# The transfers of the last two blocks' turned results: from two queues to one

## The chip, the cores and the metric

The kernel runs on one core of a Trainium2 chip. The metric is the device time of one execution in microseconds (us). Before the change it is 588.04 us, the median of 3 runs (587.76 to 588.65).

## The reference

Attention over packed keys, and then a channel mix on what it gives. Eight batches of 8 heads, 576 tokens and 64 values per head are read; 4608 tokens of 512 channels are written.

```python
p_packed = sm_attn(p, k, v)                 # 32 packed rows attend to 576 tokens
x = sm_attn(q, p_packed, p_packed)          # 576 tokens attend to the 32 rows
# x: (8, 576, 512) after the heads are put side by side
xk = mu_k * x + (1.0 - mu_k) * x_prev       # x_prev: the token before
xr = mu_r * x + (1.0 - mu_r) * x_prev
k = np.maximum(xk @ w_k, 0.0)               # 512 -> 1024
v = k * k @ w_v                             # 1024 -> 512
r = 1.0 / (1.0 + np.exp(-(xr @ w_r)))       # 512 -> 512
return (r * v).astype(np.float32)
```

## The kernel before

The 4608 tokens are cut into nine blocks of 512. Blocks 0 to 6 go through the channel mix one after the other (gates, keys, values), and their results have tokens on the partitions, so that each goes to `out` in rows. The last two blocks (`PAIR`, blocks 7 and 8) are worked on together: keys and values of the pair are made in seven products of halves in place of eight, and in these the channels are on the partitions and the 512 tokens along the free dimension. So a result of theirs must be turned before it can be written.

That end of the kernel is `values_of_pair` (L1716). Its table `passes` (from L1777) has seven passes named A11, S2, S3, S1, A12, S4 and A22. A pass fills two PSUM banks (j = 0 and 1) with 12 matmuls each: 4 chunks of weights, and for each chunk a product of high parts and two with a low part (L1802 to L1804). Four of the passes (S1, A12, S4 and A22) end in results, two each, so there are eight results of 128 channels by 512 tokens. `made_of` (L1734) makes a result. In S1, A12 and S4 VectorE adds a kept partial sum to the bank (L1747), multiplies by the gate (L1750) and turns the result in blocks of 32 by 32 (L1752) back into the tile of the gate. In the last pass, A22, there is no partial sum to add (`n is None`); the gate is multiplied in (L1741), and the turned result goes to another tile, `turned`.

A turned result leaves in four transfers (a = 0 to 3), one for each 32 partitions: 32 partitions of 16 runs of 32 numbers, so 64 KB in 512 runs of 128 bytes. `to` and `what` in the code are their two ends. `load` (L215) issues a transfer on SyncE's queue (SP in the profile, L221). ScalarE (ACT) has a queue of its own, on which L1761 issues.

What sets the order. The kernel is written as generators, which the class `Flow` runs (L149). A generator yields an engine and an estimated time, and the planner goes on with the one that can start earliest on its engine by its own count of times. The instructions of an engine come out in the order in which the planner emits them, and each engine takes its own strictly in that order. For transfers `Flow` keeps a count named "queue", which is SP's, and one named "dma". The transfers that L1761 issues are entered under "scalar". A transfer raises a semaphore when its data has landed. There are eight of these for the transfers of SP and ACT together (DMAHW0 to DMAHW7 in the order below), dealt in turn in the order of emission, and before a transfer is issued its engine waits until the one that had the same semaphore before has landed.

Of the kernel before, what the change touches and what calls it, by code (L numbers as in the profile page):

```python
# [173 lines left out]
def attn_pack_channel_mix(ctx: ExitStack, tc: tile.TileContext, q, k, v, p, mu_k, mu_r, w_k, w_v, w_r, out):  # L174
    nc = tc.nc
# [24 lines left out]
    def vec(n, after=None):  # L200
        return "vector", 0.07 + 1.04e-3 * n, after, None
# [4 lines left out]
    def act(n, after=None, table=None):  # L206
        return "scalar", 0.14 + 0.72e-3 * n, after, table
# [4 lines left out]
    def pe(us, after=None):  # L212
        return "tensor", us, after, None

    def load(dst, src, issue, us, beside=False):  # L215
        if beside:
            yield "gpsimd", 0.6, None, None
            nc.gpsimd.dma_start(dst, src)
            return
        yield "queue", issue, None, None  # L220
        nc.sync.dma_start(dst, src)  # L221
        begin = max(flow.free.get("dma", 0.0), flow.t + 0.46)
        flow.free["dma"] = begin + us
        flow.free["queue"] = max(flow.free["queue"], begin - 2.0)
        flow.now.t = begin + us + LANDS
# [27 lines left out]
    def banks(slot):  # L253
        return ps.tile([P, 2, 512], F32, name="pa", tag=f"pa{slot}")
# [186 lines left out]
    def back_to_issue():  # L441
        flow.now.t = flow.free["queue"]
# [905 lines left out]
    def small_tile(slot, dtype, name):  # L1348
        tag, j = slot
        o = LEAD[tag][j]  # L1350
        return tile_([P, S], dtype, tag, j, name)[:, o:o + WP]
# [364 lines left out]
    def values_of_pair():  # L1716

        first, second = PAIR
        ms = []
        for _ in range(4):  # L1720
            ms.append((yield from flow.take("m")))
        Z, Y = ([ps.tile([P, TB], F32, name="pv", tag=f"m{slot}") for slot in ms[n:n + 2]] for n in (0, 2))
        X = [None, None]
        parts_of = {}

        def kept(n, j):
            slot = yield from flow.take("keep")
            x = small_tile(slot, F32, "kept")
            parts_of[n, j] = slot, x
            yield act(TB)  # L1730
            nc.scalar.copy(x, Z[j])
            flow.set(("kept v", n, j))

        def made_of(bank, j, i, h, n):  # L1734
            yield from flow.wait(("sig", i, 2 * h + j))
            sig = sigs[i, 2 * h + j]
            if n is None:
                slot = yield from flow.take("keep")
                x = small_tile(slot, F32, "turned")
                yield vec(TB)  # L1740
                nc.vector.tensor_tensor(sig, bank[j], sig, op=ALU.mult)  # L1741
                sig, x = x, sig
            else:
                yield from flow.wait(("kept v", n, j))
                slot, x = parts_of[n, j]
                yield vec(TB)
                nc.vector.tensor_tensor(x, bank[j], x, op=ALU.add)  # L1747
                flow.set(("read v", n, j))
                yield vec(TB)
                nc.vector.tensor_tensor(x, x, sig, op=ALU.mult)  # L1750
            yield vec(TB)
            nc.vector.transpose(sig.rearrange("p (a b) -> p a b", b=32), x.rearrange("p (a b) -> p a b", b=32))  # L1752
            if n is not None:
                flow.give("keep", slot)
            for a in range(4):
                d = DH * h + P * j + 32 * a
                to = out[i * TB:(i + 1) * TB, d:d + 32].rearrange("(b k) i -> k b i", k=32)
                what = sig[32 * a:32 * a + 32].rearrange("k (b i) -> k b i", i=32)
                if n is None and a % 2:
                    yield "scalar", 0.1, None, None  # L1760
                    nc.scalar.dma_start(to, what)  # L1761
                else:
                    yield from load(to, what, 0.5, 0.3)
                    back_to_issue()

        def of_wv(f0, o):
            return lambda u, j: tuple(wvs[f0 + u][:, x, o + j * P:o + (j + 1) * P] for x in range(2))

        def of_wr(home):
            flat = home.rearrange("p c d -> p (c d)").rearrange("p (h u d) -> p h u d", h=2, u=HF)  # L1770
            return lambda u, j: tuple(flat[:, x, u, j * P:(j + 1) * P] for x in range(2))

        def of_wk(u, j):
            o = DH * (u % 2) + j * P
            return tuple(x[:, u // 2, o:o + P] for x in (wk_h, wk_l))

        passes = (  # L1777
            ("A11", None, of_wv(0, 0), Z, True, None, lambda j: kept("P1", j)),
            ("S2", T2, of_wr(wr_h), Z, False, ("kept v", "P1"), lambda j: kept("U2", j)),
            ("S3", T3, of_wr(wr_l), Z, False, ("kept v", "U2"), lambda j: kept("U3", j)),  # L1780
            ("S1", T1, of_wv(0, DH), X, True, None, lambda j: made_of(X, j, second, 1, "U3")),
            ("A12", None, of_wv(HF, 0), Y, True, None, lambda j: made_of(Y, j, first, 0, "P1")),
            ("S4", None, of_wv(HF, DH), X, False, ("read v", "U3"), lambda j: made_of(X, j, first, 1, "U2")),
            ("A22", T4, of_wk, Z, False, ("kept v", "U3"), lambda j: made_of(Z, j, second, 0, None)),
        )
        for name, weights_, ws, bank, opens, before, evict in passes:
            if weights_:
                yield from flow.wait(("tv", weights_))
            if bank[0] is None:
                for j in range(2):  # L1790
                    X[j] = banks((yield from flow.take("pa")))[:, 0, :]
            for j in range(2):
                if before:
                    yield from flow.wait((*before, j))
                for u in range(HF):
                    yield from flow.wait(("vf", name, u))
                    slot, xh, xl = forms_v[name, u]
                    yield pe(0.685)
                    flow.now.t -= flow.LAG
                    wh, wl = ws(u, j)  # L1800
                    go = not opens
                    nc.tensor.matmul(bank[j], wh, xh, start=(opens and u == 0), stop=False, skip_group_check=go)  # L1802
                    nc.tensor.matmul(bank[j], wh, xl, start=False, stop=False, skip_group_check=go)  # L1803
                    nc.tensor.matmul(bank[j], wl, xh, start=False, stop=(u == HF - 1), skip_group_check=go)  # L1804
                    if j:
                        flow.give("ring", slot)
                flow.spawn(evict(j), 0, flow.t + flow.LAG)
# [98 lines left out]
```

## Time and profile before

| what | value |
|---|---|
| time, median of 3 | 588.04 us |
| the profiled execution's own time | 586.39 us |
| its span | 584.6 us |
| TensorE's granted clock, mean | 0.994 |
| PE / VectorE / ScalarE busy | 97% / 75% / 60% |
| transfers on SP's queue | 41.0% of 16 engines' span |
| transfers on ACT's queue (q10) | 2112 packets, 0.26 MB |

How to read it: the profile is of one execution, whose time lies 1.65 us under the median of the runs; its span covers all but 1.8 us of that time. PE is busy nearly throughout, so nearly all of the span is its work. The page's 40 slices are 14.6 us each, and in the last of them PE is busy for 2 tenths and the transfers go on. The chain of waits names TensorE, VectorE and ScalarE; what comes after the last of their instructions are transfers, and these are read from the timeline of SP and ACT and from what each of these waited for.

### The profile page before, as it was taken

What the parts mean: (1) busy time and instruction counts of PE and PEld (TensorE: products, weight loads), DVE (VectorE), ACT (ScalarE), POOL (GpSimd) and SP (SyncE); (2) the same over time, 40 slices, a digit from 0 to 9 for tenths busy, and PEclk for the clock granted to TensorE, in tenths of its full rate; (3) what the DMA queues carried; (4) which work ended last, traced back from release to release, by engine and by line L of the source; (5) the groups of instructions that cost most, each with busy time, mean ns of one, the idle gap of its engine ahead of it and who ended that gap; (6) DMA issues with size and microseconds to landing.
All of it is one profiled execution on the core that took longest, in us unless ns stands there. A gap on an engine that the chain in (4) does not pass through costs nothing.

```text
span 584.6 us, 10714 instructions
## 1 busy us (share of the span) xinstructions
PE 567.9 (97%) x4067; PEld 447.1 (76%) x4067; DVE 435.7 (75%) x804; ACT 349.0 (60%) x625; POOL 13.2 (2%) x41
## 2 busy tenths in 40 slices
PE   8999999899999999999999999999999999999992
PEld 7877777687788778877877777777788888888881
DVE  1999789956892889088829788559896985858991
ACT  5678983765744584268427752746568755578710
POOL 3000000000000000000000000000000100100000
PEclk9999999999999999999999999999999999999997
DMA  8987440863366364407640763730122340600034
GB/s 304 339 244 230 112 66 11 191 143 59 76 134 169 49 142 91 146 5 153 117 127 16 155 141 102 158 98 1 64 82 73 110 161 19 217 0 1 1 64 81
DMA packets 182612, 65.08 MB, mean 111 GB/s; under 512 B 154008, under 2 KB 172576, under 8 KB 182304
## 3 DMA queue, kind: packets, MB, share of 16 engines
q1 hardware_dynamic: 178208, 59.80, 41.0%
q0 software_dynamic: 2240, 4.33, 2.5%
q8 instruction: 32, 0.52, 0.4%
q10 hardware_dynamic: 2112, 0.26, 0.3%
q14 instruction: 20, 0.16, 0.1%
HBM read 47.19 MB, written 17.17 MB: 110 GB/s over the span
## 4 chain that ended last, share of the span: by engine, by line
PE 78%; DVE 12%; ACT 4%; issue 2%; DMA 1%; SPq 0%; POOL 0%; DVEq 0%; POOLq 0%; ACTq 0%
PE ph L1162 8%; PE ph L1163 7%; PE ph L1164 7%; PE pvo L1244 7%; PE pvo L1245 7%; PE pvo L1246 7%; PE pr L1214 4%; PE pr L1216 4%; PE pr L1215 3%; PE pa L706 2%; DVE x L1117 2%; PE pv L1804 2%; PE pv L1802 2%; PE pv L1803 2%; PE pa L898 1%
## 5 line engine op out<-in xcount | busy, mean ns | idle before, releaser
L1162 PE MATMUL ph<-xk,wk_h 128*128 128x512 f32 x224 | 90.8, 405 | 0.0
L1244 PE MATMUL pvo<-wv,sq 128*128 128x512 f32 x224 | 89.0, 397 | 0.0
L1163 PE MATMUL ph<-xk,wk_h 128*128 128x512 f32 x224 | 87.6, 391 | 0.0
L1164 PE MATMUL ph<-xk,wk_l 128*128 128x512 f32 x224 | 87.4, 390 | 0.0
L1245 PE MATMUL pvo<-wv,sq 128*128 128x512 f32 x224 | 87.4, 390 | 0.0
L1246 PE MATMUL pvo<-wv,sq 128*128 128x512 f32 x224 | 87.3, 390 | 0.0
L1174 ACT ACTIVATE r<-ph 128x512 f32<-128x512 f32 x56 | 33.6, 600 | 46.5 <-PE ph L1164 44.5
L1162 PEld LDWEIGHTS ph<-xk,wk_h 128*128 128x128 f32 x224 | 42.1, 188 | 14.2 <-issue 5.9
L1244 PEld LDWEIGHTS pvo<-wv,sq 128*128 128x128 f32 x224 | 42.1, 188 | 13.6 <-issue 4.9
L1117 DVE SCALAR_TENSOR_TENSOR x<-xt,mus,x 128x128 f32<-128x128 f32 (+6 forms) x100 | 46.5, 505 | 4.0 <-ACT x L1111 3.8
L1164 PEld LDWEIGHTS ph<-xk,wk_l 128*128 128x128 f32 x224 | 42.1, 188 | 9.0
L1246 PEld LDWEIGHTS pvo<-wv,sq 128*128 128x128 f32 x224 | 42.1, 188 | 8.9
L1245 PEld LDWEIGHTS pvo<-wv,sq 128*128 128x128 f32 x224 | 42.1, 188 | 8.1
L1111 ACT ACTIVATE x<-xt,mus 128x128 f32<-128x128 f32 (+6 forms) x100 | 47.6, 523 | 1.2 <-DVE sq L1190 1.2
L1163 PEld LDWEIGHTS ph<-xk,wk_h 128*128 128x128 f32 x224 | 42.2, 188 | 7.6 <-DVE xk L1056 0.2
L1214 PE MATMUL pr<-wr_h,xr 128*128 128x512 f32 x112 | 45.4, 405 | 0.7 <-ACT xr L1137 0.7
L1216 PE MATMUL pr<-wr_h,xr 128*128 128x512 f32 x112 | 43.9, 392 | 0.8 <-DVE xr L1139 0.8
L1190 DVE TENSOR_TENSOR sq<-r,sq 128x512 fp32r<-128x512 f32 x56 | 38.0, 678 | 8.8 <-ACT sq L1185 4.8
L1215 PE MATMUL pr<-wr_l,xr 128*128 128x512 f32 x112 | 43.8, 391 | 0.0
L1072 ACT COPY xt<-pa 128x576 f32<-128x576 f32 x28 | 30.6, 1174 | 10.8 <-PE pa L898 10.7
L1177 ACT ACTIVATE r<-r 128x512 f32<-128x512 f32 x56 | 35.5, 634 | 1.2
L1188 DVE CAST sq<-r 128x512 fp32r<-128x512 f32 x40 | 16.7, 417 | 22.5 <-ACT r L1177 21.9
(266 smaller groups left out, 1071.8 us busy)
## 6 DMA issues: line engine op xcount, KB each, us to landing
vt<-in_v SPq DMA_DIRECT2D x14, 512.0 KB, 4.5
raw<-in_k SPq DMA_DIRECT2D x96, 72.0 KB, 2.7
raw<-in_q SPq DMA_DIRECT2D x96, 72.0 KB, 2.7
out<-sig SPq DMA_DIRECT2D x23, 256.0 KB, 2.7
st<-in_moe_w_k SPq DMA_DIRECT2D x8, 512.0 KB, 9.5
st<-in_moe_w_v SPq DMA_DIRECT2D x8, 512.0 KB, 5.6
far<-at SPq DMA_DIRECT2D x12, 288.0 KB, 2.6
aTd<-far SPq DMA_DIRECT2D x12, 256.0 KB, 2.9
```

The costliest lines, as they stand in the source:

```text
L1111: nc.scalar.mul(x32[:, o:o + n], xts[b, c][:, 1 + s:1 + s + n], mus[:, j, c:c + 1])
L1117: nc.vector.scalar_tensor_tensor(x32[:, o:o + n], xts[b, c][:, s:s + n], mus[:, j + 1, c:c + 1], x32[:, o:o + n], op0=ALU.mult, op1=ALU.add,)
L1162: nc.tensor.matmul(ph, wk_h[:, c, fs], xh, start=(c == 0), stop=False)
L1163: nc.tensor.matmul(ph, wk_h[:, c, fs], xl, start=False, stop=False)
L1164: nc.tensor.matmul(ph, wk_l[:, c, fs], xh, start=False, stop=(c == NC - 1))
L1190: nc.vector.tensor_tensor(hl[:, 1, :], r, hl[:, 0, :].bitcast(F32), op=ALU.subtract)
L1214: nc.tensor.matmul(pr, xh[:, ts_], wr_h[:, c, :], start=(c == 0), stop=False)
L1215: nc.tensor.matmul(pr, xh[:, ts_], wr_l[:, c, :], start=False, stop=False)
L1216: nc.tensor.matmul(pr, xl[:, ts_], wr_h[:, c, :], start=False, stop=(c == NC - 1))
L1244: nc.tensor.matmul(pv[t], sh, wvs[f][:, 0, :], start=(f == 0), stop=False)
L1245: nc.tensor.matmul(pv[t], sh, wvs[f][:, 1, :], start=False, stop=False)
L1246: nc.tensor.matmul(pv[t], sl, wvs[f][:, 0, :], start=False, stop=(f == NF - 1))
```

## The change

In `made_of`, the branch that sent every second transfer of the last pass's results through ScalarE's queue is taken out. All 32 transfers of the eight results now go through `load`.

```diff
                 what = sig[32 * a:32 * a + 32].rearrange("k (b i) -> k b i", i=32)
-                if n is None and a % 2:
-                    yield "scalar", 0.1, None, None
-                    nc.scalar.dma_start(to, what)
-                else:
-                    yield from load(to, what, 0.5, 0.3)
-                    back_to_issue()
+                yield from load(to, what, 0.5, 0.3)
+                back_to_issue()
```

Apart from line numbers the instructions of TensorE, VectorE and GpSimd are the same in the same order, and so are SP's and ACT's up to the places below.

SP before, from the first transfer of the third result. The results in the order in which they are made are `sig_5419`, `sig_5446`, `sig_5469`, `sig_5493`, `turned_6164` and `turned_6184` (two of S1, `sigs`, come ahead of them); in brackets stands what an instruction waits for, DMAHW being the semaphore of an earlier transfer and DVE the VectorE.

```order
L221 DMA out<-sig_5419 32x16x32 [waits DMAHW6_49,DVE_49]
L221 DMA out<-sig_5419 32x16x32 [waits DMAHW7_49]
L221 DMA out<-sig_5419 32x16x32 [waits DMAHW1_49]
L221 DMA out<-sig_5419 32x16x32 [waits DMAHW3_49]
L221 DMA out<-sig_5446 32x16x32 [waits DMAHW5_49,DVE_49]
L221 DMA out<-sig_5446 32x16x32 [waits DMAHW7_49]
L221 DMA out<-sig_5446 32x16x32 [waits DMAHW0_49]
L221 DMA out<-sig_5446 32x16x32 [waits DMAHW1_49]
L221 DMA out<-sig_5469 32x16x32 [waits DMAHW2_49,DVE_49]
L221 DMA out<-sig_5469 32x16x32 [waits DMAHW3_49]
L221 DMA out<-sig_5469 32x16x32 [waits DMAHW4_49]
L221 DMA out<-sig_5469 32x16x32 [waits DMAHW5_49]
```

The semaphores 0, 2, 4 and 6 are skipped in the first six of these rows, and they are the ones that ACT's transfers have.

ACT before, the end of its instructions.

```order
L1710 CAST hl_6060<-q_5590 128x512 [waits PE_49,Activation_49]
L1710 CAST hl_6087<-q_5590 128x512 [waits PE_49,Activation_49]
L1761 DMA out<-turned_6164 32x16x32 [waits DMAHW0_49,DVE_49]
L1761 DMA out<-turned_6164 32x16x32 [waits DMAHW2_49]
L1761 DMA out<-turned_6184 32x16x32 [waits DMAHW4_49,DVE_49]
L1761 DMA out<-turned_6184 32x16x32 [waits DMAHW6_49]
```

By their semaphores these four were emitted among the transfers of `sig_5419` and the first two of `sig_5446`; now they are gone from ACT, and its last instruction is the cast of `hl_6087`.

SP now, from the same row as above.

```order
L221 DMA out<-sig_5419 32x16x32 [waits DMAHW6_49,DVE_49]
L221 DMA out<-sig_5419 32x16x32 [waits DMAHW7_49]
L221 DMA out<-sig_5419 32x16x32 [waits DMAHW0_49]
L221 DMA out<-sig_5419 32x16x32 [waits DMAHW1_49]
L221 DMA out<-sig_5446 32x16x32 [waits DMAHW2_49,DVE_49]
L221 DMA out<-sig_5446 32x16x32 [waits DMAHW3_49]
L221 DMA out<-sig_5446 32x16x32 [waits DMAHW4_49]
L221 DMA out<-sig_5446 32x16x32 [waits DMAHW5_49]
L221 DMA out<-sig_5469 32x16x32 [waits DMAHW6_49,DVE_49]
L221 DMA out<-sig_5469 32x16x32 [waits DMAHW7_49]
L221 DMA out<-sig_5469 32x16x32 [waits DMAHW0_49]
L221 DMA out<-sig_5469 32x16x32 [waits DMAHW1_49]
```

The eight semaphores now come in turn, so that each of SP's transfers waits for the one of its own queue eight issues earlier; this goes on in the same way through `sig_5493` and the eight transfers of the two `turned` tiles, four rows more than before.

## Rows read from the trace of the kernel before

**Rows 1.** The page: span, then the chain of waits from 572.9 us on (start, us).
```profile
span 584.6 us, 10714 instructions
...
572.98 0.24 PE pv L1804
573.22 0.02 issue
573.24 0.70 DVE sigs L1741
573.95 0.02 issue
573.97 0.71 DVE turned L1752
```

**Rows 2.** Timeline of SP's queue, by stretches (start us, us from first to last).
```profile
560.67 2.01 SPq L221 DMA_DIRECT2D out<-sigs  x4
...
563.16 3.01 SPq L221 DMA_DIRECT2D out<-sig  x6
...
573.80 1.96 SPq L221 DMA_DIRECT2D out<-sig  x4
...
576.66 3.02 SPq L221 DMA_DIRECT2D out<-sig  x6
...
579.79 0.97 SPq L221 DMA_DIRECT2D out<-turned  x2
...
581.17 0.85 SPq L221 DMA_DIRECT2D out<-turned  x2
```

**Rows 3.** What SP waited for, 566 to 574 us, and 575 to 582 us.
```profile
SPq L221 <- DMA out<-turned: 7.6, 1, 7.6
...
SPq L221 <- DMA out<-turned: 0.9, 1, 0.9
```

**Rows 4.** Timeline of ACT's queue, 571 to 573 us and 574 to 577 us.
```profile
571.99 0.93 ACTq L1761 DMA_DIRECT2D out<-turned  x2
...
574.71 0.95 ACTq L1761 DMA_DIRECT2D out<-turned  x2
```

**Rows 5.** Issues of short windows: KB each, median us to landing (571.9, 574.6 us).
```profile
out<-turned ACTq DMA_DIRECT2D x1, 64.0 KB, 1.8
...
out<-turned ACTq DMA_DIRECT2D x1, 64.0 KB, 1.9
```

**Rows 6.** Timeline of VectorE, 562.4 to 575 us: the turns.
```profile
562.42 0.71 DVE L1752 STREAM_TRANSPOSE sig<-kept 128x512 f32<-128x512 f32 x1
...
564.47 0.71 DVE L1752 STREAM_TRANSPOSE sig<-kept 128x512 f32<-128x512 f32 x1
...
566.54 0.71 DVE L1752 STREAM_TRANSPOSE sig<-kept 128x512 f32<-128x512 f32 x1
...
569.26 0.71 DVE L1752 STREAM_TRANSPOSE sig<-kept 128x512 f32<-128x512 f32 x1
...
571.25 0.71 DVE L1752 STREAM_TRANSPOSE turned<-sigs 128x512 f32<-128x512 f32 x1
```

**Rows 7.** Single issues: timeline of SP at 562.2 us and 581.5 us.
```profile
562.19 0.49 SPq L221 DMA_DIRECT2D out<-sigs  x1
...
581.53 0.48 SPq L221 DMA_DIRECT2D out<-turned  x1
```

**Rows 8.** Us to landing: stretches 560.6 to 563 us, 573.7 to 576 us, 581.05 to 584.6 us.
```profile
out<-sigs SPq DMA_DIRECT2D x4, 64.0 KB, 1.9
...
out<-sig SPq DMA_DIRECT2D x4, 64.0 KB, 2.2
...
out<-turned SPq DMA_DIRECT2D x2, 64.0 KB, 2.1
```

**Rows 9.** All 32 issues to `out`, 545 to 590 us: their times to landing.
```profile
DMA to landing us min/median/max: 1.7/1.9/3.9
```

**Rows 10.** Stretches of the end: engines' busy us, granted clock, DMA share, GB/s.
```profile
566.17:573.80 7.63, 7.04 (x32) 5.49 (x30) 5.10 (x8) 0.00 (x0) 0.00 (x0) 1.00 0.19 33
...
575.76:576.66 0.90, 0.00 (x0) 0.00 (x0) 0.00 (x0) 0.00 (x0) 0.00 (x0) 1.00 1.02 172
576.66:581.99 5.33, 0.00 (x0) 0.00 (x0) 0.00 (x0) 0.00 (x0) 0.00 (x0) 0.55 0.69 117
```

## The prediction

> **What bounds the kernel now.** I read the chain of waits first, at its end. The last instruction of a computing engine is VectorE's turn of the last result, 573.97 + 0.71 = 574.68 us, and the span is 584.6 us [rows 1]. So 9.9 us at the end hold no computation; nothing but transfers of results that are made already is left. Before that PE runs at the full clock almost without a gap (7.04 of 7.63 us in the stretch up to 573.8 us, the rest being after its last matmul) [rows 10], and neither its instructions nor VectorE's change. The question is thus only when the last transfer lands.
>
> Next I read SP's queue there. From 560.67 us on it issues 24 transfers, in six pieces [rows 2]. The second piece, of six, is the four of `sig_5419` and two of `sig_5446`; it ends at 563.16 + 3.01 = 566.17 us. Then SP issues nothing for 7.63 us, until 573.80. Yet VectorE made results all that time: its turns end at 563.13, 565.18, 567.25, 569.97 and 571.96 us [rows 6], and the last at 574.68 [rows 1]. So when SP resumes, the third and fourth transfers of `sig_5446` have been ready for 8.6 us, and eight of the two next results and two of the first `turned` one stand behind them. From 573.80 on SP works off 14 transfers with little pause, and its last issue starts at 581.53 [rows 7], 6.9 us after the last result was ready.
>
> What held SP is named in its waits: a transfer of `turned`, once for 7.6 and once for 0.9 us [rows 3]. SP has not yet issued any of `turned` then, so it is one of ACT's. ACT issues the first of them at 571.99, as soon as the turn of the fifth result is done [rows 4, 6]; it takes 1.8 us to land [rows 5], 573.8, and SP goes on at 573.80. The same again: ACT's third is issued at 574.71 and takes 1.9, so 576.6, and SP's pause from 575.76 ends at 576.66 [rows 2, 4, 5]. The order shows why: the third transfer of `sig_5446` waits for DMAHW0, and the third of `sig_5469` for DMAHW4, which ACT's first and third hold. They were dealt to ACT before SP's rows, but ACT cannot issue until results exist that are made some 7 us later. A queue that is taken strictly in order thus waits for a result newer than the one it is to write.
>
> **The change, part by part.** Gone are both waits. Each of SP's transfers now waits for the landing of the one eight issues ahead on its own queue. Eight issues are two results; two results take at least 4.1 us to be made [rows 6], and a landing takes 1.7 to 3.9, median 1.9 us [rows 9], so these waits are met before their turn.
>
> Added are four issues on SP, moved from ACT; ACT does nothing after them, so nothing gets free there. Price of a result with four issues in a row after a wait: 2.01 us; six in a row cost 3.01 and 3.02, so again 0.50 each [rows 2]. The results come 2.05, 2.07, 2.72, 1.99 and 2.72 us apart [rows 1, 6]. Going through them: `sig_5419` is issued at 563.16 to 565.1 and `sig_5446` from 565.20 on as before; its four end near 567.2. `sig_5469` is ready at 567.25 and ends near 569.3. `sig_5493`, ready at 569.97, ends near 572.0. The first `turned`, ready at 571.96, ends near 574.0, and now all four of its transfers are on SP. The last result is ready at 574.68 and finds the queue empty. There is 0.7 us of slack there; the last four would begin late only if a result's issue cost over (574.68 - 569.97) / 2 = 2.36 us.
>
> So the end: the last four begin at 574.71, as ACT's first of that result did [rows 4]; they take 2.01 us, and the last issue starts 0.49 us before the end of that, at 576.23 [rows 2, 7]. It lands 1.9 us later, as after the like four from 560.67 on [rows 8], at 578.13. The span now ends 584.6 - (581.53 + 2.1) = 1.0 us after the last landing [rows 1, 7, 8], and I keep that. End: 579.1 us. The gain is 584.6 - 579.1 = 5.5 us, of which 5.3 is the earlier last issue and 0.2 the landing. Against the profiled execution's own 586.39 us that makes 580.9; that execution lies 1.65 us under the median of the runs, 588.04, and taken from the median it is **582.5 us**, 0.94% faster.
>
> Bounds of the unknown terms. The four issues of the last result on one queue: from 1.96 to 2.01 us in a row of four [rows 2], and 0.4 more if a pause like that between 580.76 and 581.17 [rows 2], whose cause the profile doesn't name, falls into them. The landing: 1.7 to 2.2 us, 2.2 being that of four issued while ACT's were under way, with the 16 engines at their full share, 1.02 [rows 8 to 10]; I take 1.9, since nothing else is on the way then. The 3.9 was a single early one and is left aside. Together the profile's end lies between 578.9 and 579.9, so the gain between 4.7 and 5.7 us. One more doubt is that without the profiler an issue may cost less than 0.5 us. If it cost nothing, the old end would be set by the landing of ACT's third at 576.66 and one more landing, the new one by 574.71 and one landing: still 1.95 us, the least gain that this mechanism allows. ACT's queue has no other transfer in this kernel, so whatever a second queue costs at the start or end goes too; no row shows such a cost, and I take nothing.
>
> What ACT's queue gave the last result is lost: its two issues on each queue side by side are 0.95 us long [rows 4] against 2.01 for four on one [rows 2], so 1.06 us. That is in the sum above already. The Trainium skill speaks for the old form here: in "DMA: Bandwidth & Descriptors", section "Issuing engines are not separate DMA queues", it says that starting transfers on several engines saves only the sequencers' time to start them, as all run on the same 16 DMA engines. By that rule alone the change would give back those 1.06 us and gain nothing, 589.1 us. The trace agrees that there is issue time to save, but SP's two waits on ACT's landings cost more.
>
> **The rivals.**
> First, less is gained: an issue costs less outside the profile, or the last four meet a pause and land late. With issues at 0.25 us the ten issues after 576.66 now would take 2.5 us and the four after the change 1.0, a gain of about 3.4 us: 584.6. For it: the median is 1.65 us over the profiled execution, so the two are not alike in everything. Against it: the pace of 0.5 us goes with 117 GB/s of packets that keep the 16 engines 69% busy when SP is alone [rows 10], and that work doesn't depend on the profiler.
>
> Second, slower: the 7.63 us are not ACT's landing but something in SP's queue itself that ends near 573.8 whatever it waits for, and the profile's releaser is a coincidence. Then 18 transfers in place of 14 follow 573.80. The four more cost 4 x 0.50 = 2.0 us, and the second pause of 0.9 falls away: 1.1 us later, 589.1; if that pause stays as well, 590.0. It decides from the point at which SP's third transfer of `sig_5446` starts after 573 us. Against it: the order puts exactly the first row that waits for an ACT transfer at that place, and both pauses end within 0.1 us of an ACT landing [rows 2, 4, 5].
>
> Third, no change within what counts: something other than SP's transfers ends the span a little after 583 us. No engine has work there [rows 10], so I see no candidate.
>
> **How the numbers follow.** Forecast, gain of 4.5 to 6 us: 0.85. Smaller gain, 1.9 to 4.5 us: 0.10. Slower: 0.03. No change: 0.02. A difference under 0.2%, 1.2 us, cannot be told from no change here. Even the least gain of the mechanism, 1.95 us, is over that, so faster has 0.95, same 0.02 and slower 0.03. The likeliest case alone reaches from 582.0 to 583.5; the runs of before spread over 0.9 us, and with part of the smaller gain the range is 581.4 to 584.4.
>
> **What would show it.** Right: SP's queue shows no pause over 1 us that a transfer of `turned` ends; each result's four issues begin within 0.1 us of its turn; the last issue starts near 576.2 and the span ends near 579.1, with the last turn at 574.7 as before; ACT issues nothing. Wrong: SP still silent between 566 and 573 us, the last four starting after 575, landings of over 2.5 us there, or an end more than 1.5 us after the last landing.

## The result, and the profile after

The changed kernel takes 581.35 us, the median of 4 runs (580.91 to 581.86), beside 587.9 us for the kernel before (4 runs): a ratio of 0.989, with a 95% interval from 0.988 to 0.991. The forecast was 582.5 us. A second comparison with more runs of before (below) gave 581.1 us beside 586.89.

The chain of waits and the turns come first, as in [rows 1, 6]: what feeds the end of the changed kernel (the last turn, then the three before it). Columns are start in us, then duration.

```profile
span 579.5 us, 10712 instructions
...
574.34 0.71 DVE turned L1752
```

```profile
566.90 0.71 DVE L1752 STREAM_TRANSPOSE sig<-kept 128x512 f32<-128x512 f32 x1
...
569.62 0.71 DVE L1752 STREAM_TRANSPOSE sig<-kept 128x512 f32<-128x512 f32 x1
...
571.62 0.71 DVE L1752 STREAM_TRANSPOSE turned<-sigs 128x512 f32<-128x512 f32 x1
```

The computing engines do what they did, 0.37 us later: the last turn ends at 575.05 instead of 574.68 us. The matmuls are as many, and the delay comes long before the changed place: 0.1 us by 16 us and the rest between 349 and 367 us. In a second profile of the changed kernel (below) the last turn ends at 574.86, so it is one execution against another. It has to be taken off in every comparison of profiles here, and I count times from the end of the last turn. From there to the end of the span it was 9.9 us; now it is 579.5 - 575.05 = 4.4.

SP's queue in the changed kernel, to be laid beside [rows 2], in stretches; then its waits from 566 to 574.9 us, beside [rows 3].

```profile
563.52 8.78 SPq L221 DMA_DIRECT2D out<-sig  x16
...
572.41 0.96 SPq L221 DMA_DIRECT2D out<-turned  x2
...
573.72 0.85 SPq L221 DMA_DIRECT2D out<-turned  x2
...
575.08 1.94 SPq L221 DMA_DIRECT2D out<-turned  x4
```

```profile
SPq L221 <- DVE sig L1752: 0.5, 1, 0.5
```

The two pauses of 7.6 and 0.9 us, ended by a transfer of `turned`, are gone. In that stretch SP waits 0.5 us in all, for VectorE, which is how a queue should wait that keeps up with its producer. The sixteen transfers of the four `sig` results, spread before over 16.5 us (563.16 to 579.68), take 8.78. The last four begin 0.03 us after the last turn (575.08). Where the time went by stretches, as in [rows 10] (busy us of PE, its weight loads, VectorE, ScalarE, GpSimd; granted clock, DMA share, GB/s): the 7.7 us in which SP stood still before now move data at 117 GB/s, where they moved 33.

```profile
566.50:574.20 7.70, 7.07 (x32) 5.52 (x30) 5.17 (x8) 0.00 (x0) 0.00 (x0) 1.00 0.68 117
```

The last issue starts at 576.52, the landing takes the usual 1.9 (at 578.42 in the trace), and 1.0 us later, at 579.45, the span ends (issue, and then KB and us to landing of the last four):

```profile
576.52 0.49 SPq L221 DMA_DIRECT2D out<-turned  x1
...
out<-turned SPq DMA_DIRECT2D x4, 64.0 KB, 1.9
```

### The profile page after: what moved, and what is told of

It reads as the page before. It is cut to its first block, busy times and chain, and to the rows that moved or that the text cites. A ratio compares the mean times of both kernels' runs of the same rounds, so it can differ in the third digit from the quotient of the medians.

```text
span 579.5 us, 10712 instructions
## 1 busy us (share of the span) xinstructions
PE 568.2 (98%) x4067; PEld 447.0 (77%) x4067; DVE 435.7 (75%) x804; ACT 349.2 (60%) x625; POOL 13.3 (2%) x41
## 4 chain that ended last, share of the span: by engine, by line
PE 80%; DVE 11%; DMA 3%; ACT 2%; issue 1%; SPq 1%; DVEq 0%; ACTq 0%
PE ph L1162 8%; PE ph L1163 8%; PE ph L1164 8%; PE pvo L1244 7%; PE pvo L1245 7%; PE pvo L1246 7%; PE pr L1214 4%; PE pr L1216 4%; PE pr L1215 4%; PE pa L706 2%; DVE x L1117 2%; DMA st<-in_moe_w_r 2%; PE pv L1799 2%; PE pv L1798 2%; PE pv L1800 2%; PE pa L898 1%
```

## Experiments

My theory: SP stood still because one of its transfers had to wait for a semaphore that ACT's transfer of a newer result held. The rivals: ACT's queue as such costs (by the number of its transfers, or at the end), or SP pauses for a reason of its own. All kernels here start from the one before and differ in a line or two of `made_of`.

**A second queue without that wait.** ACT gets half of every result, so the two queues go through the results side by side and no transfer waits for one of a newer result.

```diff
-                if n is None and a % 2:
+                if a % 2:
```

> Second and fourth transfers of all eight turned results go to ACT's queue (in before: of the last two results alone), so that both queues take the results in the order in which they are made and no transfer waits for one of a newer result. Theory (a transfer on SP that waits for a newer result's transfer on ACT is what cost the time, not ACT's queue as such): no pause of SP that a transfer of turned ends, last four issues side by side near 574.7 to 575.7, the last landing near 577.5, span 578.4 to 579.2, time 5.5 to 7.5 us under before, and 0.3 to 0.8 us under the changed kernel. Rival (issuing from ACT itself disturbs SP or the end): 587 to 590, like before.

Measured: 581.41 us beside 586.87 (ratio 0.991, 0.989 to 0.992). With 16 transfers on ACT in place of 4 the loss of 5.5 us is gone just the same, so it was not ACT's queue. SP's waits from 562 to 574.9 us are for VectorE alone:

```profile
SPq L221 <- DVE sig L1752: 5.6, 4, 1.8
SPq L221 <- DVE turned L1752: 1.1, 1, 1.1
```

The gain on before is at the lower edge of the 5.5 to 7.5 us expected. The part on the changed kernel (0.3 to 0.8 us under it) did not come; that is taken up with the last experiment.

**A second queue with semaphores of its own.** The same four transfers as in before, but by GpSimd, whose transfers have other semaphores (DMASW).

```diff
-                    nc.scalar.dma_start(to, what)
+                    nc.gpsimd.dma_start(to, what)
```

> As before, the second and fourth transfers of the last two results leave by a second queue, but it is GpSimd's, whose transfers have semaphores of their own. Theory: SP has no pause of several us between 566 and 574, since none of its transfers waits for one of GpSimd's; SP's last issue starts near 575.3. The end is then set by GpSimd's two last transfers, whose price no row shows: with 1 to 2 us an issue and 2 to 3 to land, span 579.5 to 583, time 2 to 6 us under before. Rival (a second queue at the end costs by itself, or SP pauses for a reason of its own): SP still silent from 566 to 573.8, time within 1 us of before or over it.

Measured: 581.57 us (ratio 0.991, 0.990 to 0.993), span 580.1. SP's waits up to 574.9 us, and GpSimd's two last issues:

```profile
SPq L221 <- DVE sig L1752: 1.0, 2, 0.5
```

```profile
575.43 1.29 POOL L1761 DMA_DIRECT2D out<-turned  x2 [1.37 <-DVE turned L1752]
```

Which transfers leave by another queue, and when they are ready, is as in before; the engine that issues them is another, and they share no semaphore with SP's. ACT as such is already ruled out by the kernel above, so it is the shared semaphores that make the pause. GpSimd's issue took 0.65 us and not 1 to 2: no row shown ahead has its price, but the trace of before has it, at 0.5 to 0.8 us for GpSimd's other transfers.

**Moving the newer result.** If SP's pause ends with the landing of a certain result of ACT's, it must move when that result is another. First ACT gets two transfers of the last result only, then two of the last but one only. Each time that is half as many as in before.

```diff
-                if n is None and a % 2:
+                if n is None and j and a % 2:
```

> Only the last result's second and fourth transfers are on ACT, so half as many as in before; by the order SP's third transfer of sig_5469 now waits for the first of them. Theory: SP pauses until that one has landed, 574.7 + 1.9 = 576.6, with 12 transfers left; last issue starts near 576.6 + 11 x 0.51 = 582.2, span 584.9 to 585.7, so slower than before by 0.3 to 1.1 us and slower than the changed kernel by 5 to 8 us. Rival (the cost goes by the number of transfers on ACT, or is SP's own): half of the loss, 584 to 585, or the changed kernel's time.

Measured: 587.77 us (ratio 1.0017, 1.0008 to 1.0026), so slower than before with half the transfers on ACT. Its SP waits from 566 to 582 us, its ACT, and SP after the pause:

```profile
SPq L221 <- DMA out<-turned: 8.2, 1, 8.2
```

```profile
575.29 0.93 ACTq L1761 DMA_DIRECT2D out<-turned  x2
```

```profile
577.10 3.02 SPq L221 DMA_DIRECT2D out<-sig  x6
580.22 3.50 SPq L221 DMA_DIRECT2D out<-turned  x6
```

The pause now ends at 577.10, 1.8 us after ACT's issue of the last result, with 12 transfers left. The span is 586.2, that is 10.9 us after the last turn (575.25), where it was 9.9 in before. The last issue was at 583.24, a microsecond later than expected: 0.6 of it is the later turn, the rest SP's pause from 581.22 to 581.58 and an issue of 0.67 in place of 0.5.

```diff
-                if n is None and a % 2:
+                if n is None and not j and a % 2:
```

> Only the last but one result's second and fourth transfers are on ACT. By the order SP's first transfer of sig_5469 waits for the first of them. Theory: SP pauses until 572.0 + 1.8 = 573.8 with 14 transfers left and no second pause: last issue near 573.8 + 13 x 0.53 = 580.7, span 583.3 to 584.0, so faster than before by 0.6 to 1.3 us and slower than the changed kernel by 4 to 6 us. Rival (number of transfers on ACT): the same time as with the last result's alone, within 0.5 us.

Measured: 586.34 us (ratio 0.9991, 0.9982 to 0.9999). The same views:

```profile
SPq L221 <- DMA out<-turned: 6.5, 1, 6.5
```

```profile
571.93 0.92 ACTq L1761 DMA_DIRECT2D out<-turned  x2
```

```profile
573.79 4.11 SPq L221 DMA_DIRECT2D out<-sig  x8
578.00 3.31 SPq L221 DMA_DIRECT2D out<-turned  x6
```

Now it ends at 573.79, again 1.86 us after the issue on ACT that it waits for, and 14 transfers follow, the last from 580.83 on. The gain over before, 0.5 us, is a little under the 0.6 to 1.3 expected. The last issue came as expected (580.7), but the last transfers took 2.2 to 2.6 us to land; why is not shown. The number of transfers on ACT is the same in these two, and they differ by 1.4 us; the rival by number falls. The rival that SP pauses by itself falls too, for the pause ends where ACT's transfer lands: at 573.8 in before, 573.8 with the last but one result and 577.1 with the last.

**The size, and the faster version that I hoped for.** The changed kernel and the one with half of every result on ACT, on one chip.

> The changed kernel once more, for the size of the gain, with many runs of before beside it. If the profiled executions tell the gain rightly (span 584.6 to 579.5, 5.1 us; 5.5 us with the last turn at the same place), it is 5.0 to 5.8 us; if the 6.5 us of the first comparison hold, something outside the profile gains another microsecond, and it is 6.2 to 6.9 us.

> The kernel with half of every turned result's transfers on ACT, beside the changed kernel on one chip. In its profile the last landing comes 0.4 us sooner after the last turn than in the changed kernel, and its end checks 0.4 us longer. If the landing decides, 0.3 to 0.6 us under the changed kernel; if the longer end eats it, within 0.2 us of it.

Measured: 581.1 us for the changed kernel beside 586.89 (ratio 0.990, 0.989 to 0.991), 581.58 for the other (0.991, 0.989 to 0.992). The gain is 5.8 us, at the upper edge of the 5.0 to 5.8 that the profiled executions gave. Its interval, 5.1 to 6.7 us, doesn't exclude the 6.5 of the first comparison, but there the median of before was a microsecond above those of the thirty later runs. Of the two cases expected for the half-and-half kernel neither came by the medians: here it is 0.5 us longer, and 581.41 beside 581.35 above. But its runs (580.98 to 581.81) overlap those of the changed kernel (581.03 to 581.24), so the two can't be told apart. The last four transfers of the half-and-half kernel on each queue, and the times to landing of its transfers of `turned` from 574.9 us on:

```profile
575.34 0.85 SPq L221 DMA_DIRECT2D out<-turned  x2
```

```profile
575.34 0.93 ACTq L1761 DMA_DIRECT2D out<-turned  x2
...
DMA to landing us min/median/max: 2.2/2.3/2.5
```

The four are issued in 0.93 us instead of 1.94, as [rows 4] had it, so the last issue ends 1.0 us sooner after the turn. But they land after 2.2 to 2.5 us, where the changed kernel's have 1.7 to 1.9; the last landing comes 0.4 us sooner. In both profiles of this kernel the time from the last landing to the end is then 1.4 us, where both of the changed kernel have 1.0. The trace shows what lies in it. After the last landing (578.26) SP goes through the semaphores of its last transfers one by one, and from 578.40 to 578.75 it stands still, with no semaphore to wait for; in the changed kernel no such gap follows the last landing. This is the short pause of SP that the prediction could not place: in the changed kernel it comes earlier, where slack covers it. It takes back 0.35 of the 0.4 us, so the hoped-for gain was lost there. No run moves that pause, so this is read from the traces and not tested.

## Why the prediction was right

The mechanism and its steps. All that it said of SP's queue came about: both waits gone, each result's four begun within 0.1 us of its turn or of the end of the four ahead, the queue empty when the last result comes, ACT issuing nothing. The experiments show that it is the wait for the newer result's semaphore, and not the queue.

The terms. For the last result 2.01 us were taken and 1.94 came, for the landing 1.9 and 1.9, for the rest 1.0 and 1.0. Start of the last four after the last turn: 0.03 us, as taken. From the last turn to the end that makes 4.4 us by the forecast (579.1 - 574.68) and 4.4 measured. The gain, 5.5 us, is 5.1 in the two spans, 5.5 with the drift of the compute taken off, and 5.8 in the runs.

The pause of 0.4 us that might have fallen into the last four did not. It is there again, from 573.37 to 573.72, and stands at the same place in SP's queue as before: after the eighteenth transfer counted from the first of `sig_5419`. In the changed kernel that is in the last but one result, whose four still end at 574.56, 0.5 us ahead of the last turn. In before it stood in the path, so 0.35 us of the gain come from its move. That it fell there and not into the last four was luck: the forecast took its last four without it, but had no reason for its place. Both kernels of the moved result have it after the eighteenth too. What fixes the place is told in the last section.

Where it was off. The time, 582.5, was taken from a median of 588.04 us out of three runs. Thirty later runs of before have medians of 586.87 (21 runs) and 586.89 (9), so this was a microsecond high, and the sum made on the profiled execution, 580.9, was nearer to the measured 581.1 to 581.35. These two lie just under the lower end of the stated range, 581.4, though the gain that was forecast, 5.5 us, is nearly what came. With that goes the argument for the first rival, that the profiled execution (586.39) and the runs were not alike: it lies within the runs' spread (586.23 to 588.65).

What stands ahead says that the semaphores are dealt in the order of emission. That is not exact. In `made_of` a result's first transfer is emitted on SP before its second is on ACT, and still ACT's had semaphore 0 ahead of SP's transfers of results up to four places earlier. By what order they are dealt instead is not shown by any run here. For the time it made no difference, since the forecast was read from the waits in the order itself.

The rule of the Trainium skill weighed there ("DMA: Bandwidth & Descriptors", section "Issuing engines are not separate DMA queues") says that several issuing engines save only issue time. The half-and-half kernel agrees: 1.0 us of issue is saved, of which slower landings gave back 0.6. By the rule alone the change would have lost that time; what it leaves out is that the queues here were tied to each other by semaphores, which cost 5.5 us.

## What to carry to other kernels

Where two queues share a small set of completion semaphores, look in the order at which transfer had the semaphore before: if it belongs to a result made later, the queue stands still until then, and everything behind it too. The sign in a trace is a queue that is silent while its results lie ready, and whose pause ends one landing after an issue on another queue. Either keep such transfers on one queue, share out every result alike, or use a queue with its own semaphores: all three came to the same time here.

## What the runs showed of the hardware that was not expected

Four transfers of 64 KB in runs of 128 bytes gain 1.0 us of issue on two queues, but only 0.4 us in the last landing. GpSimd issues such a transfer in 0.65 us, against some 0.5 on SP, and its last two landed after 2.3 us, as ACT's do beside SP.

SP's short pause has a fixed place in its program. In each of the eight traces SP stands still five times with no semaphore to wait for, 0.34 to 0.45 us each: ahead of the 80th, 208th, 336th, 464th and 592nd of its instructions in the trace, so every 128 instructions. Outside these places it never does so for more than 0.07 us. After each of them, within 2 us, a transfer of 8 KB starts on the queue that carries instructions (q14); after the last of them it is the only one there from 546 us on. That fits an engine which gets its program in pieces of 128 instructions, but no run here tests it. Where the 592nd falls decides what the pause costs: in the changed kernel it falls into slack, in before between the last issues and in the half-and-half kernel behind the last landing, both in time that counts.
